# A long convolution rebuilt as a pipeline over 5 channel blocks, with taps as diagonal matmuls and a router that stays on the chip

## The chip, the cores and the metric

The kernel runs on one core of one Trainium2 chip. The engines of a core work side by side, each in its own program order: TensorE (PE, matmuls into PSUM), VectorE (DVE), ScalarE (ACT), GpSimd (POOL) and SyncE (SP, which here only issues DMAs). They wait for one another by semaphores. The metric is the device time of one execution in microseconds (us); the kernel before took 339.98 us, the median of 3 runs (338.54 to 340.74).

## The reference, cut to what matters

There are 2048 tokens of 640 channels, bf16. Part A is a gated long convolution between two modulated layer norms, part B a small expert that is applied to the 8 tokens with the highest router score.

```python
mod = (_silu(c) @ w_mod)                    # six vectors: sa, ca, ga, sb, cb, gb
h = _layernorm(x) * (1 + ca) + sa           # x = A_q
# part A
for t in range(4):                          # 4 shift taps along the tokens
    k_shift += k_pad[:, t:t + S, :] * shift_k[:, 3 - t]
kv = k_shift * v
y  = irfft(rfft(pad(kv)) * rfft(pad(ssm_k)))[:S] + kv * ssm_D   # length 4096, per channel
x = x + ga * (h * y)
h = _layernorm(x) * (1 + cb) + sb
# part B
r = h @ w_r;  idx = the 8 largest r
y = (silu(h[idx] @ w_gate) * (h[idx] @ w_up)) @ w_down * sigmoid(r[idx])
x = x + gb * (h + scatter_add(y, idx))
```

## The kernel before

Tokens lie 16 to a partition (`(p m) d`), so a full array is `[128, 16, 640]` bf16, 20 KB a partition. All big arrays share one pool of 7 such slots (tag `b20`). A scheduler orders each engine's instructions by their dependences and the slots; DMAs go out from SP's queue, the expert's weights and the last scatter from POOL's.

The Fourier transform of length 4096 is done in two steps of matmuls with a transposition through DRAM between them, for two halves of 320 channels. The sine tables `Cf`, `Sf` are made on the chip (L116 to L149) and transposed on PE (L156). `modv`, the six modulation vectors on all partitions, comes from 40 matmuls (L214). `ssm_k` is turned around through DRAM (`Gd`, `gL`, L282 to L286).

`kv` is made on DVE alone (L357 to L367): for each of 16 token groups four products with a tap, three sums and the product with `v`. `F1` (L288) is the first transform step: 64 matmuls a source, evicted by ACT with a rearrangement into `gZS` or `ZS`. `T1` (L298) stores that to `Zd` in DRAM and loads it back with a DMA transpose. `F3` (L306) is the second step, evicted by ACT and DVE. The spectra X and H are multiplied on DVE, 24 operations a half (L436 to L441). `I1` and `I2` (L324, L340) are the inverse steps. The first layer norm makes `h` on DVE (L393 to L415) beside the second half of the transforms; `h` goes to DRAM (`h_scr`) and comes back.

Then the tail: x1 = x + h*y (L461, L462), `layernorm` (L229) with sums on ACT and the rest on DVE and ACT, the router scores on DVE (L472), written to DRAM and read back as one row of 2048 on one partition, `max` and `max_index` there (L486, L488), the one-hot selection by matmuls (L514), the two projections (L529), the down projection (L550), the output on DVE (L561, L562), two stores, and an indirect DMA that adds the 8 rows to the stored output.

Of the kernel before, what the change touches and what calls it, by code (L numbers as in the profile page):

```python
# [19 lines left out]
M2 = 16  # L20
FF = 1728
NSEL = 8
NFFT = 4096
EPS = 1e-5
HB = 40
HC = 320


def _kernel_body(ctx, tc, A_q, A_k, A_v, A_shift_k, A_ssm_k, A_ssm_D,
                 B_w_r, B_w_gate, B_w_up, B_w_down, c, w_mod, out, dbg=None):  # L30
    nc = tc.nc
    dbg = dbg or {}

    def dump(name, ap):
        if name in dbg:
            nc.sync.dma_start(out=dbg[name], in_=ap)

    const = ctx.enter_context(tc.tile_pool(name="const", bufs=1))
    small = ctx.enter_context(tc.tile_pool(name="small", bufs=2))
    one = ctx.enter_context(tc.tile_pool(name="one", bufs=1))  # L40
    big = ctx.enter_context(tc.tile_pool(name="big", bufs=7))
    psum = ctx.enter_context(tc.tile_pool(name="psum", bufs=4, space=bass.MemoryType.PSUM))
    psum2 = ctx.enter_context(tc.tile_pool(name="psum2", bufs=2, space=bass.MemoryType.PSUM))
    dram = ctx.enter_context(tc.tile_pool(name="dram", bufs=1, space=bass.MemoryType.DRAM))

    def B20(name, shape, dtype=BF):
        n = 1
        for s_ in shape[1:]:
            n *= s_
        assert n * mybir.dt.size(dtype) <= 20480, (name, shape)  # L50
        return big.tile(list(shape), dtype, name=name, tag="b20")

    xq_d = A_q.flatten_outer_dims().rearrange("(p m) d -> p m d", p=P)
    k_d = A_k.flatten_outer_dims()
    k_d3 = k_d.rearrange("(p m) d -> p m d", p=P)
    v_d = A_v.flatten_outer_dims().rearrange("(p m) d -> p m d", p=P)
    out_d = out.flatten_outer_dims().rearrange("(p m) d -> p m d", p=P)

    cT = const.tile([P, 5], F32, name="cT")
    cT_bf = one.tile([P, 5], BF, name="cT_bf")  # L60
    D5 = one.tile([P, 5], BF, name="D5")
    with nc.allow_non_contiguous_dma(reason="tiny transposed loads"):
        nc.sync.dma_start(out=cT_bf[:], in_=c.rearrange("o (t p) -> p (o t)", p=P))
        nc.sync.dma_start(out=D5[:], in_=A_ssm_D.rearrange("(q r) -> q r", r=5))
    shk_bc = one.tile([P, 4, D], BF, name="shk_bc")
    kh = one.tile([P, 3, D], BF, name="kh")
    wr_bc = const.tile([P, D], BF, name="wr_bc")
    nc.sync.dma_start(out=wr_bc[:], in_=B_w_r.partition_broadcast(P))
    nc.vector.tensor_copy(out=cT[:], in_=cT_bf[:])

    trig_slot = B20("trig_slot", [P, 10240])
    trig_t = trig_slot[:, 0:5120].bitcast(F32).rearrange("p (a b) -> p a b", a=5)
# [563 lines left out]
```

## Time and profile before

| | |
|---|---|
| median of 3 runs | 339.98 us (338.54 to 340.74) |
| profiled execution, from its first to its last instruction | 336.5 us |
| mean granted clock of TensorE | 0.744 |
| DMA packets | 59888, 60.23 MB, mean 179 GB/s |

The slices of the page cut the span into 40 pieces; here are the other engines, the granted clock and the DMA share in tenths.

```profile
PE   0004900005776688929407795077500000002962
ACT  3111678004998598715403495024899677000000
POOL 5110000000000000000000000021000000000001
PEclk9999965555999569976957998559965555555859
DMA  6999382759167999999109703479910000000330
```

Four stretches can be read from them. Up to about 57 us, tables, loads and modulation; from there to 157 us the taps and the forward transforms; to 237 us products and inverse transforms; from then on the tail, in which PE and the DMA engines are nearly idle until 308 us.

### The profile page before, as it was taken

What the parts mean: (1) busy time and instruction counts of PE and PEld (TensorE: products, weight loads), DVE (VectorE), ACT (ScalarE), POOL (GpSimd) and SP (SyncE); (2) the same over time, 40 slices, a digit from 0 to 9 for tenths busy, and PEclk for the clock granted to TensorE, in tenths of its full rate; (3) what the DMA queues carried; (4) which work ended last, traced back from release to release, by engine and by line L of the source; (5) the groups of instructions that cost most, each with busy time, mean ns of one, the idle gap of its engine ahead of it and who ended that gap; (6) DMA issues with size and microseconds to landing.
All of it is one profiled execution on the core that took longest, in us unless ns stands there. A gap on an engine that the chain in (4) does not pass through costs nothing.

```text
span 336.5 us, 2691 instructions
## 1 busy us (share of the span) xinstructions
PE 137.7 (41%) x811; PEld 75.4 (22%) x811; DVE 248.5 (74%) x582; ACT 157.0 (47%) x275; POOL 11.7 (3%) x24
## 2 busy tenths in 40 slices
PE   0004900005776688929407795077500000002962
PEld 0002400002332234403106652056300000001631
DVE  5999880999999504897994429955860499999832
ACT  3111678004998598715403495024899677000000
POOL 5110000000000000000000000021000000000001
PEclk9999965555999569976957998559965555555859
DMA  6999382759167999999109703479910000000330
GB/s 219 431 405 428 152 297 93 263 118 204 80 253 307 240 289 258 345 257 392 78 0 161 152 1 111 202 263 406 381 51 0 0 0 1 0 1 3 156 158 1
DMA packets 59888, 60.23 MB, mean 179 GB/s; under 512 B 52906, under 2 KB 55090, under 8 KB 57698
## 3 DMA queue, kind: packets, MB, share of 16 engines
q1 hardware_dynamic: 58706, 53.42, 49.7%
q0 software_dynamic: 1168, 6.65, 5.1%
q8 instruction: 6, 0.10, 0.1%
q14 instruction: 8, 0.07, 0.1%
HBM read 28.59 MB, written 18.36 MB: 140 GB/s over the span
## 4 chain that ended last, share of the span: by engine, by line
DVE 54%; PE 16%; ACT 10%; DMA 9%; issue 6%; another core or an unknown queue 3%; SPq 1%; POOLq 1%; DVEq 0%
DVE ks_acc L366 6%; DVE ks_prod L365 6%; DVE acc_junk L472 4%; ACT ln_junk L235 3%; DMA xq<-in_A_q_dram 3%; PE ps_i L331 2%; PE ps_i L330 2%; DMA gZT<-Zd 2%; DMA ZT<-Zd 2%; PE pxs L514 2%; DVE ks_acc L362 2%; DVE ln_t L271 2%; DVE h L272 2%; DVE kv L367 2%
## 5 line engine op out<-in xcount | busy, mean ns | idle before, releaser
L330 PE MATMUL ps_i<-RA,Y 128*128 128x256 bf16 x80 | 21.6, 308 | 27.0 <-DVE Y L438 24.0
L336 ACT CAST UT<-ps_i 128x512 bf16<-128x512 f32 x20 | 11.7, 586 | 43.7 <-PE ps_i L331 27.8
L493 PE MATMUL pbc<-mif,ones 1*128 1x8 f32 x2 | 0.6, 351 | 67.3 <-DVE mif L490 67.3
L292 PE MATMUL ps_f<-gL,Cf 128*128 128x320 bf16 x32 | 10.8, 338 | 41.3 <-DMA gL<-Gd 36.6
L296 ACT CAST gZS<-ps_f 128x640 bf16<-128x640 f32 x32 | 19.8, 693 | 14.4 <-PE ps_f L293 14.4
L338 DVE CAST UT<-ps_i 128x512 bf16<-128x512 f32 x20 | 13.8, 692 | 14.9 <-ACT UT L336 14.9
L331 PE MATMUL ps_i<-RB,Y 128*128 128x256 bf16 x80 | 21.5, 308 | 3.6 <-DVE Y L441 3.6
L366 DVE TENSOR_TENSOR ks_acc<-ks_acc,ks_prod 128x640 bf16<-128x640 bf16 x48 | 22.9, 481 | 0.0
L296 ACT CAST ZS<-ps_f 128x640 bf16<-128x640 f32 x32 | 20.2, 693 | 5.2 <-PE ps_f L293 5.2
L365 DVE TENSOR_TENSOR ks_prod<-kt,shk_bc 128x640 bf16<-128x640 bf16 x45 | 20.4, 481 | 0.0
L320 DVE CAST H<-ps_f3i 128x480 bf16<-128x480 f32 (+1 forms) x12 | 7.5, 625 | 17.0 <-PE ps_f3i L318 17.0
L293 PEld LDWEIGHTS <-Sf 128*128 128x128 bf16 x64 | 6.5, 101 | 59.4 <-issue 59.2
L315 ACT CAST X<-ps_f3r 128x480 bf16<-128x480 f32 (+1 forms) x22 | 12.2, 554 | 11.7 <-PE ps_f3r L314 10.7
L330 PEld LDWEIGHTS <-Y 128*128 128x128 bf16 x80 | 11.7, 148 | 25.4 <-DVE Y L438 24.7
L493 PEld LDWEIGHTS pbc<-mif,ones 1*128 1x128 f32 x2 | 0.5, 304 | 67.6 <-issue 67.6
L269 ACT ACTIVATE ln_t<-ln_t,ln_rs 128x640 bf16<-128x640 bf16 x16 | 13.1, 827 | 5.2 <-DVE ln_t L266 3.7
L292 PE MATMUL ps_f<-kv,Cf 128*128 128x320 bf16 x32 | 11.6, 361 | 8.1 <-DVE kv L367 4.3
L320 DVE CAST X<-ps_f3i 128x480 bf16<-128x480 f32 (+1 forms) x12 | 7.5, 624 | 9.7 <-PE ps_f3i L318 9.7
L331 PEld LDWEIGHTS <-Y 128*128 128x128 bf16 x80 | 11.8, 148 | 9.9 <-issue 4.7
L315 ACT CAST H<-ps_f3r 128x480 bf16<-128x480 f32 (+1 forms) x22 | 12.2, 558 | 3.7 <-issue 2.0
L156 PE MATMUL pt_trig<-ident,Cf 128*128 128x128 bf16 x16 | 2.2, 286 | 27.4 <-ACT Cf L130 27.4
L348 ACT ACTIVATE ys<-ps_i 128x640 bf16<-128x640 f32 x16 | 10.4, 701 | 3.9 <-PE ps_i L346 3.9
(188 smaller groups left out, 479.0 us busy)
## 6 DMA issues: line engine op xcount, KB each, us to landing
xq<-in_A_q_dram SPq DMA_DIRECT2D x2, 2560.0 KB, 10.1
Zd<-gZS SPq DMA_DIRECT2D x4, 1280.0 KB, 4.8
Zd<-ZS SPq DMA_DIRECT2D x4, 1280.0 KB, 5.8
g_sb<-in_A_ssm_k_dram SPq DMA_DIRECT2D x1, 2560.0 KB, 16.1
kt<-in_A_k_dram SPq DMA_DIRECT2D x1, 2560.0 KB, 33.0
vt<-in_A_v_dram SPq DMA_DIRECT2D x1, 2560.0 KB
Gd<-g SPq DMA_DIRECT2D x1, 2560.0 KB, 14.3
h_scr<-h SPq DMA_DIRECT2D x1, 2560.0 KB, 7.5
```

The source lines that it names most:

```text
L269: nc.scalar.activation(out=t4[:], in_=t1[:], func=ACT.Copy, scale=rs[:, m:m + 1])
L292: nc.tensor.matmul(ps[:, 0, 0:HC], lhsT=Cf[:, m2, :], rhs=src[:, m2, col0:col0 + HC], start=True, stop=True)
L296: nc.scalar.copy(out=o_ap, in_=i_ap)
L315: nc.scalar.copy(out=dst[:, 0, k0:k0 + nk, :].rearrange("p a b -> p (a b)"), in_=psr[:, 0:ncol])
L320: nc.vector.tensor_copy(out=dst[:, 1, k0:k0 + nk, :].rearrange("p a b -> p (a b)"), in_=psi[:, 0:ncol])
L330: nc.tensor.matmul(o, lhsT=Yt[:, 0, :, blk], rhs=RA[:].rearrange("p a b -> p (a b)"), start=True, stop=False)
L331: nc.tensor.matmul(o, lhsT=Yt[:, 1, :, blk], rhs=RB[:].rearrange("p a b -> p (a b)"), start=False, stop=True)
L336: nc.scalar.copy(out=o_ap, in_=i_ap)
L338: nc.vector.tensor_copy(out=o_ap, in_=i_ap)
L365: nc.vector.tensor_tensor(out=prod[:], in0=src, in1=shk_bc[:, j, :], op=ALU.mult)
L366: nc.vector.tensor_tensor(out=acc[:], in0=acc[:], in1=prod[:], op=ALU.add)
L472: nc.vector.scalar_tensor_tensor(out=junk[:], in0=h2[:, m, :], scalar=1.0, in1=wr_bc[:], op0=ALU.mult, op1=ALU.mult, accum_out=r32[:, m:m ...
```

## The change

The program is written anew. Channels go in 5 blocks of 128 (`NB`), tokens along the free dimension for the taps (`kT`, `vT`, loaded by DMA transpose, two for each block) and 128 tokens to a partition group for the norms (`(m p) d`). SP's and POOL's instructions keep the order in which they are written; the scheduler still orders PE, DVE and ACT.

For a block `b`, `conv(b)` makes the taps as 16 matmuls of 512 columns with diagonal matrices that hold a tap, and DVE multiplies the PSUM result by `vT`. The block goes to DRAM and comes back in another order (`kvd`, `xA`). `stage_A` and `stage_B` are the two transform steps, for two sources at a time that share one pair of buffers `A` and `HX`: g0 with g1, g2 with kv0, g3 with kv1, g4 with kv2, kv3 with kv4. `product` multiplies two spectra in place with 12 DVE operations. `stage_BT` and `stage_AT` are the inverse steps, with a trip through DRAM (`Ud`, `uA`) between them. `stage_AT` adds h*y to x, and takes the statistics and the router score of the block at once, the score by transposing x on PE and multiplying it by two columns of weights. Norm and score are finished when all blocks are in. `Balance` gives a set share of the PSUM evictions to DVE and the rest to ACT. PSUM is one pool of four buffers of two banks. `HX` has three buffers, which in turn hold the angles for the tables, the spectra and a part of `w_mod`; another part of `w_mod` lies where x is loaded later.

The top 8 are found for 16 groups of 128 tokens on 16 partitions, and the 128 candidates are ranked by comparisons; nothing of it goes through DRAM. The output is summed on PE by three matmuls with the identity and evicted by ACT.

```diff
-        nc.vector.tensor_tensor(out=kv[:, m, :], in0=acc[:], in1=vt[:, m, :], op=ALU.mult)
+    ctx.enter_context(tc.manual_schedule(engines={mybir.EngineType.SP, mybir.EngineType.Pool}))
+    psum = ctx.enter_context(tc.tile_pool(name="psum", bufs=4, space=bass.MemoryType.PSUM))
...
+    def conv(b):
+        for i2 in range(2):
+            ps = ps_tile([P, 2, 512])
+            for i in range(2):
+                n0 = 16 + 512 * (2 * i2 + i)
+                for j in range(4):
+                    nc.tensor.matmul(ps[:, i, :], lhsT=diag_b(b)[:, j, :], rhs=kT[:, n0 - j:n0 - j + 512],
+                                     start=(j == 0), stop=(j == 3))
+            V.tensor_tensor(out=kvT[:, 1024 * i2:1024 * i2 + 1024], in0=ps[:].rearrange("p a b -> p (a b)"),
+                            in1=vT[:, 1024 * i2:1024 * i2 + 1024], op=ALU.mult)
+        nc.gpsimd.dma_start(out=kvd[:], in_=kvT[:])
...
+    def stage_A(src, A, u):
+        for g4 in range(4):
+            ps = ps_tile([P, 2, 32, 16])
+            for bb in range(4):
+                nc.tensor.matmul(ps[:, bb // 2, :, (bb % 2) * 8:(bb % 2) * 8 + 8], lhsT=src[:, 4 * g4 + bb, :],
+                                 rhs=RA[:].rearrange("p k c e -> p (k c) e"), start=True, stop=True)
+            bal.copy(o, ps[:])
+    def stage_B(A, HX):
+        for kk in range(8):
...
+                nc.tensor.matmul(ps[:, i, :], lhsT=FT[:, 0, k2, :], rhs=f(A[:, 2 * k2:2 * k2 + 2]),
+                                 start=True, stop=False)
...
+            bal.copy(HX[:, 2 * kk:2 * kk + 2].rearrange("p k c u d -> p (k c u d)"),
+                     ps[:].rearrange("p a b -> p (a b)"))
+    def product(xt, ux, ht, uh):
+        for hk in range(2):
...
+            V.tensor_tensor(out=t0, in0=Xr, in1=Hr, op=ALU.mult)
+            V.tensor_tensor(out=t1, in0=Xi, in1=Hi, op=ALU.mult)
+            V.tensor_tensor(out=t2, in0=Xr, in1=Hi, op=ALU.mult)
+            V.tensor_tensor(out=Xi, in0=Xi, in1=Hr, op=ALU.mult)
+            V.tensor_tensor(out=Xr, in0=t0, in1=t1, op=ALU.subtract)
+            V.tensor_tensor(out=Xi, in0=Xi, in1=t2, op=ALU.add)
...
+    def stage_AT(b):
+        for hb in range(2):
...
+            V.tensor_tensor(out=t[:].rearrange("p m (g j) -> p m g j", g=2), in0=ps[:].rearrange("p g m j -> p m g j"),
+                            in1=h[:, :, cc].rearrange("p m (g j) -> p m g j", g=2), op=ALU.mult)
+            V.tensor_tensor(out=xq[:, :, cc], in0=xq[:, :, cc], in1=t[:], op=ALU.add)
+        for m in range(M):
+            V.bn_stats(out=st2[:, m, b, :], in_=xq[:, m, c0:c0 + P])
...
+        for m in range(M):
+            nc.tensor.matmul(pr[:, m, :], lhsT=xT[:, m, :], rhs=wcol[:, b, :], start=True, stop=True)
...
+    product(X1, 1, X0, 0)
+    stage_B(A2, X2)
+    stage_BT(X1, 1, 0)
...
+    product(X2, 1, X0, 1)
+    stage_B(A3, X3)
+    stage_BT(X2, 1, 1)
+    load_uA(1)
+    stage_AT(0)
+    A4, X4 = As(), HXs()
+    stage_A(kvAs[3], A4, 0)
+    stage_A(kvAs[4], A4, 1)
+    product(X3, 1, X1, 0)
+    stage_B(A4, X4)
...
+            for hf in range(2):
+                cc = slice(hf * 320, hf * 320 + 320)
+                nc.tensor.matmul(po[:, hf, 0:320], lhsT=ident[:], rhs=gbs[:, cc], start=True, stop=False)
+                nc.tensor.matmul(po[:, hf, 0:320], lhsT=ident[:], rhs=xq[:, m, cc], start=False, stop=False)
+                nc.tensor.matmul(po[:, hf, 0:320], lhsT=ident[:], rhs=tm[:, i, cc], start=False, stop=True)
+            nc.scalar.copy(out=xq[:, m, :].rearrange("p (h d) -> p h d", h=2), in_=po[:, :, 0:320])
```

Two places of the new order matter for what follows. The first is DVE's order where spectra are multiplied. Before, in the first half of the channels (T and Y are the products' buffers, X and H the spectra), the products stand by themselves:

```order
L437 TENSOR_TENSOR T_1208<-X_1118,H_786 128x1280
L439 TENSOR_TENSOR T_1208<-X_1118,H_786 128x1280
L440 TENSOR_TENSOR T_1208<-X_1118,H_786 128x1280
L438 TENSOR_TENSOR Y_1207<-T_1208 128x1280
L441 TENSOR_TENSOR Y_1207<-T_1208 128x1280
```

Now, in the product of spectra 2 and 0 (`HX_622` and `HX_170`; `Ta` and `Tb` are its buffers, `rs1` and `nm1` the norm's scale and shift, `n1a` and `n1i` steps of the scale):

```order
L265 TENSOR_TENSOR HX_622<-HX_622,Tb_760 128x8x128
L476 SCALAR_TENSOR_TENSOR nm1_954<-mv1_889,rs1_938 128x16
L260 TENSOR_TENSOR Ta_759<-HX_622,HX_170 128x1024
L479 TENSOR_SCALAR h_956<-xq_164,rs1_938,nm1_954 128x640 x16
L483 TENSOR_TENSOR h_956<-h_956,modv_163 128x2560 x2
L484 TENSOR_TENSOR h_956<-h_956,modv_163 128x2560 x2
```

All of h (16 operations, and 8 large ones, of which the last four follow below these rows) has moved between the first operation of the product's second half and its other five.

The second place is SP's queue at the loads. Before, all inputs but three go out one behind the other:

```order
L77 DMA xq_88<-in_A_q_dram 128x10240
L79 DMA g_sb_90<-in_A_ssm_k_dram 128x10240
L85 DMA wmodA_92<-in_w_mod_dram 128x5x1920
L86 DMA wmodB_93<-in_w_mod_dram 128x5x1920
L89 DMA kt_96<-in_A_k_dram 128x10240
```

Now (`wmx` and `early` are the other homes of `w_mod`, `kvd1` and `kvd2` blocks of kv in DRAM):

```order
L320 DMA xA_347<-kvd1_274 128x16x128
L338 DMA early_74<-in_w_mod_dram 128x5x640 x2
L338 DMA wmx_427<-in_w_mod_dram 128x5x640 x2
L338 DMA xq_164<-in_w_mod_dram 128x5x640 x2
L95 DMA gA_434<-in_A_ssm_k_dram 128x16x128
L83 DMA_TRANSPOSE kT_436<-in_A_k_dram 128x2048
L84 DMA_TRANSPOSE vT_437<-in_A_v_dram 128x2048
L320 DMA xA_441<-kvd2_425 128x16x128
L413 DMA xq_164<-in_A_q_dram 128x4x640 x4
```

The loads of x, once among the first, have moved behind `w_mod`, whose last two parts occupy their buffer, and behind a kv block that comes back from DRAM.

1024 lines of the change are left out of this document (530 added, 494 removed).

## The prediction

> **What bounds the kernel now.** I read the page's busy shares, the slices, the chain, then the chain in order of time and groups by form, and last the windows of the two stages that the change rebuilds.
>
> ```profile
> span 336.5 us, 2691 instructions
> PE 137.7 (41%) x811; PEld 75.4 (22%) x811; DVE 248.5 (74%) x582; ACT 157.0 (47%) x275; POOL 11.7 (3%) x24
> DVE  5999880999999504897994429955860499999832
> DVE 54%; PE 16%; ACT 10%; DMA 9%; issue 6%; another core or an unknown queue 3%; SPq 1%; POOLq 1%; DVEq 0%
> 57.00:66.00 9.00, 0.00 (x0) 0.00 (x0) 7.38 (x20) 1.09 (x2) 0.00 (x0) 0.50 0.83 299
> 75.00:84.00 9.00, 4.66 (x16) 1.98 (x16) 9.00 (x23) 3.99 (x7) 0.00 (x0) 0.50 1.01 214
> 127.00:135.00 8.00, 6.19 (x32) 3.04 (x31) 4.13 (x8) 5.93 (x13) 0.00 (x0) 1.00 1.21 262
> ```
>
> The reader is to see that VectorE (DVE) is the bound: 248.5 us busy of 336.5, 54% of the chain. The window rows give busy time of PE, weight loads, DVE, ACT, POOL, then the granted clock, the DMA share and GB/s.
>
> The change is judged by pricing its rows from these durations (start, length, what; then groups, with mean ns):
>
> ```profile
> 58.80 0.80 DVE ks_prod L365 x2
> 162.56 0.57 DVE X L320
> 165.73 0.73 DVE T L436
> 122.78 1.29 ACT ZS L296 x2
> L401 DVE BATCH_NORM_STATS2 ln_stats<-xq 128x6 f32<-128x320 bf16 x16 | 7.7, 478 | 0.0
> L402 DVE BATCH_NORM_AGGREGATE ln_mv<-ln_stats 128x2 f32<-128x12 f32 x16 | 3.1, 197 | 0.0
> 137.20 0.44 DVE L411 TENSOR_SCALAR ln_tn<-xq,ln_rstd,ln_nmr 128x640 bf16<-128x640 bf16 x1
> 137.55 0.48 DVE L415 TENSOR_TENSOR h<-ln_t,sg 128x640 bf16<-128x640 bf16 x1
> L280 DVE COPY g<-g_sb 128x2048 bf16<-128x2048 bf16 x2 | 3.9, 1995 | 0.0
> 266.64 0.17 DVE L255 TENSOR_TENSOR ln_q<-ln_t,ln_r 128x16 f32<-128x16 f32 x1
> 266.85 0.17 DVE L257 TENSOR_TENSOR ln_s<-ln_q,ln_s 128x16 f32<-128x16 f32 x1
> 184.02 0.27 PE L330 MATMUL ps_i<-RA,Y 128*128 128x256 bf16 x1
> 184.13 0.27 PE L331 MATMUL ps_i<-RB,Y 128*128 128x256 bf16 x1
> 179.64 0.42 PE L330 MATMUL ps_i<-RA,Y 128*128 128x256 bf16 x1
> 179.85 0.42 PE L331 MATMUL ps_i<-RB,Y 128*128 128x256 bf16 x1
> 317.54 2.02 PE L529 MATMUL pp_gT<-x_selT,w_gate_sb 128*128 128x8 bf16 x70 [0.27 <-DVE x_selT L521]
> ```
>
> Prices as start-to-start times. A two-operand DVE row on 640 bf16 costs 0.40 us (two in 0.80), on 1280 0.73, so 0.60 on 1024 and 1.40 on 2560. A DVE read of PSUM: 0.57 for 480, so 1.14 for 1024. ACT from PSUM: 0.645 for 640, so 0.97 for 1024, an estimate by the same slope. Statistics of 320: 0.39 after the overlap of 0.08 seen on the other rows; of 128: 0.19 by the same slope. Aggregate 0.13, two-scalar row on 640 0.35 (137.20 to 137.55), a small row that hangs on the one before 0.21. A 256-column matmul: 0.11 at clock 1, 0.21 at 0.5; 16 of them 1.75. A matmul of 8 columns: 2.02/70 = 0.029.
>
> **The change part by part.**
>
> *Removed.* The shift taps on DVE: 64 products with taps, 48 sums and 16 products with v, 128 rows at 0.40, 51 us. They become 80 matmuls of 512 columns (80 x 0.215 = 17 us of PE) and ten DVE products from PSUM (11.4 us). The second normalisation's 16 ACT pairs and its three DVE passes, and the accumulating router rows, go too:
>
> ```profile
> L235 ACT ACTIVATE ln_junk<-xq 128x640 bf16<-128x640 bf16 x16 | 11.6, 723 | 0.0
> L472 DVE SCALAR_TENSOR_TENSOR acc_junk<-h,wr_bc 128x640 bf16<-128x640 bf16 x16 | 12.1, 816 | 0.0
> L486 DVE MAX8 m<-rrow_t 1x8 f32<-1x2048 f32 x1 | 2.3, 2274 | 0.0
> ```
>
> In their place stand per block 16 statistics rows, 16 transposes and 16 two-column matmuls, and top 8 on 16 partitions x 128 instead of 1 x 2048.
>
> *All DVE rows of the new program*, priced so, come to 181 us against 248.5: evictions 26, products 60 x 0.60 = 36, first normalisation 14.6 + 17.0, five output blocks 34, the taps 11.4, tables, router and rest 42. ACT: about 79 evictions x 0.97 + 38 = 115 us. PE: 302,000 columns at 0.11/256 us = 130 us at clock 1. So DVE stays the longest engine, but no engine fills the span; the sum goes along the path.
>
> *A, start to the modulations, 60 us.* First table and first tap data at 10 (DVE's first 26 rows 6-7 us behind a first landing like the 2.7 to 3.5 us below). Then PE in its order, each step the slower of its matmuls and the evictions: four short transforms 4 x 2.9 (three ACT evictions each), four convolutions 4 x 3.5, three sine rows of ACT in the way 3, two long transforms 2 x 6.8, modulation 60 x 0.135 = 8.1: 50. DMA beside it: eight transposes, three 0.5 MB loads of g, the first kv trips, w_mod:
>
> ```profile
> 3.51 1.40 DVE L69 CAST cT<-cT_bf 128x5 f32<-128x5 bf16 x1 [3.51 <-DMA cT_bf<-in_c_dram]
> 71.01 9.94 SPq L285 DMA_TRANSPOSE gL<-Gd  x2
> wmodA<-in_w_mod_dram SPq DMA_DIRECT2D x1, 2400.0 KB, 21.6
> xq<-in_A_q_dram SPq DMA_DIRECT2D x2, 2560.0 KB, 10.1
> h_scr<-h SPq DMA_DIRECT2D x1, 2560.0 KB, 7.5
> h_re<-h_scr SPq DMA_DIRECT2D x1, 2560.0 KB, 10.5
> ```
>
> A 2560 KB transpose pair kept the SP queue 9.94 us, so 512 KB 2 us and eight 16; w_mod 21.6 as long as one half landed; the rest 5.2 MB at 10 us per 2.5 MB, 21: 59 us if nothing overlaps, 40 if they do. It is hidden by PE's 60, barely; what is late next is the modulation. Ends 46 and 72; I take 60.
> The weight on DMA has a rule against it: the Trainium skill, DMA: Bandwidth & Descriptors, section Specifications, wants at least 512 bytes in a transfer for line rate, and the loads of g and kv go in runs of 256. The trace moved its transposes, also in small packets, at 214 GB/s with the engines full, against 299 for large ones, so I keep the measured price. The rule names no rate below its bound; were it half of 214, the six such loads (3 MB, 14 us at 214) would add 14 us, an estimate, and the sum would be 272 at most.
>
> *B, the block inputs, 4 us.* x is loaded into the buffer that held w_mod, so its four loads stand on SP behind the modulation's matmuls; a quarter of 10.1 plus latency: 4.
>
> *C, DVE from the first statistics row to the last output block, 139 us.* In DVE's order the rows sum to 118.8: statistics 32 x 0.39 + 16 x 0.13 = 14.6; products 36; h 16 x 0.36 + 8 x 1.40 = 17; evictions 11.6 with the tables' and x's transposes; two tap products 2.3; five blocks each 2 x 1.14 + 2 x 0.60 + 16 x 0.19 + 0.3 = 6.8, 34; small rows 3.3. Waits on top, 20: taps of block 4 are behind the modulation on PE (4). The spectrum of block 3 takes the buffer of spectrum 0, freed only by the last product with it, and DVE has put all of h in the middle of that product; ACT's eight evictions (7.8) start then, and DVE needs the first four: 5. The block after waits for transposes, two short transforms and four evictions behind the first output block on in-order PE: 8. The last uA round trip (1 MB out, 1 MB in: 3 + 4 from the rows above) lies under two output blocks, 13.6 us: 3. Below nothing for the waits is excluded by the order; above, each could double: 0 to 40.
> *D, the tail, 52 us.* Aggregates 2, 16 small rows 3.4, 11 rows of xn 4, router 9 (fourteen small rows, four 0.73 rows that the scheduler put between them, three trips to PE), select 80 x 0.029 = 2.4 and 0.8, two projections 4.1 and 0.6, down projection 28 x 0.135 to 0.27, 5, then 96 matmuls of 320 for the output, 96 x 0.135 = 13, last ACT 0.7, last store 4, indirect add 4.2 (332.30 to the end of the span):
>
> ```profile
> 192.67 0.30 PE L345 MATMUL ps_i<-UT,Cb 128*128 128x320 bf16 x1
> 192.80 0.30 PE L346 MATMUL ps_i<-UT,Sb 128*128 128x320 bf16 x1
> 324.63 5.90 PE L550 MATMUL py<-w_down_sb,hT 128*8 128x320 bf16 x28 [3.00 <-DVE hT L544]
> 320.35 5.31 DMA out_dram<-ob
> 332.30 1.47 POOL L567 DMA_INDIRECT out_dram<-delta,idx  x1 [96.10 <-DVE delta L557]
> ```
>
> The new order puts the output matmuls behind the down projection, and the indirect add behind all four stores: 17.7 us that before lay beside the router. Ends: 44 with the output at ACT's pace alone, 65 with PE at half clock there.
>
> Sum: 60 + 4 + 139 + 52 = 255 us of span. Profiled execution 336.5, median 339.98: 3.5 around it, which stay: **258 us**.
>
> **Clock.** PE was granted 0.50 where it waited for data (57 to 84) and 1.00 where matmuls were dense (127 to 135); 256 columns took 0.21 and 0.11. I take 1 except in the tail's down projection.
> The Trainium skill, TensorE: Matmul & The Clock Gate, Part 1, says that an idle window of about 3.4 us halves the clock and a busy one restores it. The rows agree in kind; by it PE, which here waits for DVE in stages C and D, would be cold for most of them, and that is the second rival.
>
> **The rivals.**
> 1. *The waits of C are hidden and A is shorter.* For it: PE and ACT both have slack in C. Against: DVE's order. 258 - 20 - 5 = about 233.
> 2. *Half clock makes PE the bound.* PE's 39 units of 16 x 256 columns after the modulation cost 68 us at 0.11 and 134 at 0.21; half of the difference on the path, 33 us: 291. For it: 0.50 in three stretches above. Against: 1.00 wherever matmuls were denser than now.
> 3. *DVE rows on strided blocks lose the fast rate.* L280, with a step between elements, took 1995 ns for 2048, twice the time per element of ks_prod. If products, output blocks and h went so: 60 x 0.53 + 8 x 1.33 + 10 x 0.53 = 48, so 306. Against: the runs inside a row are 64 or more elements without a step.
> 4. *The round trips through DRAM are exposed: slower.* Ten trips (five of kv, five of U) hang on one in-order SP queue, behind transposes that wait for PE. With the 7.5 + 10.5 of h_scr and h_re for each, a trip is 18; if 10.5 of it showed each time, 258 + 105 - 13 of waits counted already = 350. It decides from 82/9 = some 9 us a trip. Against: each trip here is 0.5 or 1 MB, and its reader comes a block later.
> 5. *The pipeline doesn't overlap, so DVE's saving is all there is:* 340 - 67 = 273; with PE's added columns (302,000 against 227,000 by the kernel before, 75,000 at 0.11/256 us) serial on top, 305. For it: only four PSUM buffers, shared by all stages. Against: PE, DVE and ACT work on different blocks in the order that is written.
>
> **How the numbers follow.** Forecast (243 to 275) 0.55, rival 1 0.14, rival 2 0.14, rival 3 0.06, rival 4 0.05, rival 5 0.06. The time is the likeliest case's, 258. The range 236 to 298 takes in the forecast, rival 2 and most of rival 1; a third of rival 1, half of 5, and 3 and 4 lie outside, 0.19. Within 1% (337 to 343) is no change that can be told: 0.02, from the far end of 5 and the near one of 4; slower 0.05, rival 4; faster 0.93.
>
> **What would show it.** Step A: the first x load issues near 60 us. B and C: DVE at 90% or more from 64 to about 200 with two gaps of 4 to 10 us at the products with spectra 3 and 4 (ACT named). Product rows 0.60 apart. D: the output matmuls start only after the down projection, 18 us before the end. Wrong would be: gaps on DVE that name a DMA of xA or uA (rival 4), product rows above 0.9 us (rival 3), PEclk 5 through C with PE full (rival 2).

## The result, and the profile after

The new kernel takes 273.27 us, the median of 4 runs (272.77 to 273.75), beside 340.10 us for the kernel before on the same chip: a ratio of 0.806, 95% interval 0.802 to 0.809. The profiled execution has a span of 271.1 us and a time of 272.9. In all that follows, ratios leave out the slow executions of a kernel (over 1.5% above its fastest) while medians in us do not, and the profiled executions of e3 and e4 are slow ones.

The first fence is the page of the new kernel: engines, three rows of slices, the chain's shares.

```profile
span 271.1 us, 3680 instructions
PE 164.4 (61%) x1428; PEld 116.6 (43%) x1428; DVE 182.0 (67%) x443; ACT 114.3 (42%) x124; POOL 15.5 (6%) x40
DVE  5159965762477999999969219977867899502300
PEclk9999997999999965786588699959955755558995
DMA  8960999999999210500004400534889770000450
PE 38%; DVE 34%; DMA 10%; issue 10%; ACT 3%; POOL 1%; POOLq 1%; SPq 0%; DVEq 0%; ACTq 0%
```

DVE is still the longest engine, but no longer the chain's main part: 34% instead of 54. The slices show where the span isn't DVE's: the first quarter, in which the DMA engines are full, the dent after 150 us, the last fifth.

The windows of the four stages follow (start:end, length, busy time of PE, weight loads, DVE, ACT, POOL, granted clock, DMA share, GB/s): the start, the rest of stage A with B, stage C, stage D. The DMA share adds up the times of single packets, so it can come out above 1.

```profile
0.00:16.35 16.35, 0.00 (x0) 0.00 (x0) 4.84 (x22) 1.79 (x3) 3.98 (x17) 1.00 1.11 180
16.35:76.25 59.90, 53.89 (x331) 33.92 (x332) 40.05 (x71) 35.40 (x39) 2.75 (x7) 0.97 0.92 238
76.25:218.00 141.75, 83.58 (x741) 63.53 (x740) 116.43 (x271) 61.37 (x59) 7.37 (x15) 0.78 0.43 137
218.00:271.10 53.10, 26.98 (x364) 19.16 (x361) 20.66 (x81) 15.70 (x23) 1.44 (x1) 0.66 0.22 75
```

A and B together took 76.25 us where 64 were forecast, C 141.7 against 139 (116.4 of DVE rows and 25.3 of waits, against 118.8 and 20), D 53.1 against 52. DVE's sum, 182.0, met the 181 forecast.

Stage A in order of time (start, length, what; in brackets the idle time before it and what ended it):

```profile
4.71 4.45 ACTq L132 DMA_DIRECT2D cT_bf<-in_c_dram  x1
15.81 0.21 ACT L342 ACTIVATE silu_c<-cT_bf 128x5 bf16<-128x5 bf16 x1 [3.56 <-DMA cT_bf<-in_c_dram]
18.12 3.49 PE L229 MATMUL ps<-RA,gA 128*128 128x256 bf16 x16 [18.12 <-DVE gA L324]
40.95 0.23 DVE L324 TENSOR_TENSOR gA<-gA,Dt 128x16 bf16<-128x16 bf16 x1 [2.32 <-DMA gA<-in_A_ssm_k_dram]
55.93 10.73 SPq L83 DMA_TRANSPOSE kT<-in_A_k_dram  x1
60.54 2.88 PE L349 MATMUL ps<-early 128*128 128x320 bf16 x20
69.64 3.08 SPq L413 DMA_DIRECT2D xq<-in_A_q_dram  x4
76.25 0.89 DVE L471 BATCH_NORM_STATS2 st<-xq 128x6 f32<-128x320 bf16 x2 [3.35 <-DMA xq<-in_A_q_dram]
```

ACT issued two loads of g, and the issue of the small load of c behind them held the engine for 4.45 us; it landed at 15.8, and the scheduler had put the silu that needs it ahead of the first sine, from which the short table of PE's first matmul is made. So PE began at 18.1, not at 10. From there to the modulation it took 42.4 us; the forecast's steps sum to 42.2, but 3.0 of the 42.4 are a wait of PE for block 2 of g (the DVE row at 40.95), which the forecast didn't have. Then x: its loads were issued at 69.64, one us after the modulation's end and behind a transpose that had held SP's queue for 10.7 us, and their first row came 6.6 us later.

DVE's largest waits in C, the start of the next product row, and the start of stage D:

```profile
139.07 0.69 DVE L260 TENSOR_TENSOR Ta<-HX 128x1024 bf16<-128x1024 bf16 x1 [2.13 <-ACT HX L46]
155.66 1.23 DVE L44 CAST A<-ps 128x1024 bf16<-128x1024 f32 x1 [4.85 <-PE ps L229]
162.91 0.69 DVE L260 TENSOR_TENSOR Ta<-HX 128x1024 bf16<-128x1024 bf16 x1 [6.03 <-ACT HX L46]
163.52 0.68 DVE L261 TENSOR_TENSOR Ta<-HX 128x1024 bf16<-128x1024 bf16 x1
217.89 0.57 DVE L570 BATCH_NORM_AGGREGATE mv<-st 128x2 f32<-128x30 f32 x3
```

The waits stand where the forecast put them, and product rows start 0.61 us apart. The 4.85 and the 6.03 are one chain, which PE's rows of the same time show:

```profile
146.83 1.16 PE L401 MATMUL ps<-ident,xq 128*128 128x128 bf16 x16 [3.56 <-DVE xq L396]
149.99 0.59 PE L406 MATMUL ps<-wcol,xT 128*128 128x2 bf16 x16 [2.00 <-ACT xT L46]
150.44 5.62 PE L229 MATMUL ps<-RA,xA 128*128 128x256 bf16 x32
158.05 0.38 PE L240 MATMUL ps<-A,FT 128*128 128x512 bf16 x1 [2.00 <-ACT A L46]
```

PE waits for the first output block's sum (3.56), transposes it, waits for ACT's copy (2.00), computes the score, and only then starts the short transforms of kv3 and kv4 and, at 158, the long one.

### The profile page after: what moved, and what is told of

It reads as the page before. It is cut to its first block, busy times and chain, and to the rows that moved or that the text cites. A ratio compares the mean times of both kernels' runs of the same rounds, so it can differ in the third digit from the quotient of the medians.

```text
span 271.1 us, 3680 instructions
## 1 busy us (share of the span) xinstructions
PE 164.4 (61%) x1428; PEld 116.6 (43%) x1428; DVE 182.0 (67%) x443; ACT 114.3 (42%) x124; POOL 15.5 (6%) x40
## 4 chain that ended last, share of the span: by engine, by line
PE 38%; DVE 34%; DMA 10%; issue 10%; ACT 3%; POOL 1%; POOLq 1%; SPq 0%; DVEq 0%; ACTq 0%
PE ps L389 4%; DVE st L471 4%; PE ps L240 4%; PE ps L229 4%; DMA kvd<-kvT 4%; DMA gA<-in_A_ssm_k_dram 3%; DVE t L394 3%; PE ps L349 3%; PE ps L307 3%; DMA xq<-in_A_q_dram 2%; PE ps L277 2%; PE ps L677 2%; PE ps L279 2%; DVE xq L396 2%; DVE h L479 2%
## 5 line engine op out<-in xcount | busy, mean ns | idle before, releaser
L240 PE MATMUL ps<-A,FT 128*128 128x512 bf16 x80 | 33.1, 414 | 18.8 <-ACT HX L46 12.7
L46 ACT CAST HX<-ps 128x1024 bf16<-128x1024 f32 x31 | 29.9, 1023 | 32.2 <-DVE HX L263 16.9
L46 ACT CAST A<-ps 128x1024 bf16<-128x1024 f32 x30 | 28.3, 1028 | 17.9 <-PE ps L229 17.9
L229 PE MATMUL ps<-RA,gA 128*128 128x256 bf16 x80 | 14.1, 349 | 21.4 <-DVE gA L324 21.1
L242 PE MATMUL ps<-A,FT 128*128 128x256 bf16 x80 | 23.4, 293 | 0.0
L244 PE MATMUL ps<-A,FT 128*128 128x256 bf16 x80 | 23.4, 293 | 0.0
L277 PE MATMUL ps<-IT,HX 128*128 128x256 bf16 x80 | 19.8, 289 | 2.5 <-DVE HX L264 2.3
L46 ACT CAST U<-ps 128x1024 bf16<-128x1024 f32 x18 | 17.4, 1020 | 8.6 <-PE ps L279 8.0
L279 PE MATMUL ps<-IT,HX 128*128 128x256 bf16 x80 | 19.4, 289 | 0.5 <-DVE HX L265 0.5
L44 DVE CAST A<-ps 128x1024 bf16<-128x1024 f32 x10 | 12.1, 1222 | 10.9 <-PE ps L229 10.9
L307 PE MATMUL ps<-kT,early 128*128 128x512 bf16 x80 | 18.1, 379 | 0.4 <-ACT A L46 0.4
L242 PEld LDWEIGHTS <-FT 128*128 128x128 bf16 x80 | 8.4, 105 | 20.1 <-issue 18.4
L398 DVE BATCH_NORM_STATS2 st<-xq 128x6 f32<-128x128 bf16 x80 | 16.0, 280 | 0.1
L244 PEld LDWEIGHTS <-FT 128*128 128x128 bf16 x80 | 8.4, 105 | 11.2 <-issue 3.0
```

Source lines behind the costliest of these rows:

```text
L46: self.nc.scalar.copy(out=out, in_=in_)
L229: nc.tensor.matmul(ps[:, bb // 2, :, (bb % 2) * 8:(bb % 2) * 8 + 8], lhsT=src[:, 4 * g4 + bb, :], rhs=RA[:].rearrange("p k c e -> p (k c) ...
L240: nc.tensor.matmul(ps[:, i, :], lhsT=FT[:, 0, k2, :], rhs=f(A[:, 2 * k2:2 * k2 + 2]), start=True, stop=False)
L242: nc.tensor.matmul(ps[:, i, 0:256], lhsT=FT[:, 1, k2, :], rhs=f(A[:, 2 * k2 + 1:2 * k2 + 2]), start=False, stop=False)
L244: nc.tensor.matmul(ps[:, i, 256:512], lhsT=FT[:, 2, k2, :], rhs=f(A[:, 2 * k2:2 * k2 + 1]), start=False, stop=True)
L277: nc.tensor.matmul(ps[:, i, :], lhsT=xt[:, k2, 0, ux, :], rhs=IT[:, k2, 1:3, :].rearrange("p a b -> p (a b)"), start=True, stop=False)
```

## The experiments

Each kernel ran beside the kernel before, on several chips, on which that took 339.8 to 341.6 us; so ratios are compared. "Against new" is the difference of the ratios times 340 us. The three columns of stages are from the profiled executions.

| run | us, median | ratio (95%) | against new | first matmul | first statistics row | span |
|---|---|---|---|---|---|---|
| new kernel | 273.27 | 0.806 (0.802-0.809) | | 18.12 | 76.25 | 271.1 |
| e1_start | 274.92 | 0.808 (0.803-0.813) | +0.6 | 16.61 | 76.35 | 272.0 |
| e2_x_early | 281.06 | 0.823 (0.816-0.830) | +6 | 17.85 | 77.93 | 278.9 |
| e3_a4_first | 272.75 | 0.798 (0.791-0.804) | -2.8 | 18.28 | 77.82 | 273.3 |
| e4_out_spread | 266.55 | 0.777 (0.771-0.783) | -10 | 18.06 | 79.33 | 267.5 |
| e5_share0 | 270.88 | 0.795 (0.790-0.800) | -3.6 | 18.19 | 78.20 | 269.5 |
| e6_taps_dve | 290.98 | 0.852 (0.844-0.860) | +16 | 18.26 | 89.64 | 288.3 |
| e7_loads_early | 275.90 | 0.813 (0.808-0.818) | +2.4 | 15.28 | 73.49 | 272.6 |
| e8_score_later | 257.03 | 0.756 (0.752-0.759) | -17 | 18.33 | 77.21 | 254.8 |
| e9_long_runs | 271.43 | 0.796 (0.789-0.803) | -3.3 | 15.96 | 75.60 | 270.9 |
| e10_later_spread | 249.27 | 0.730 (0.724-0.736) | -26 | 18.22 | 78.89 | 247.1 |
| e11_later_spread_share0 | 248.11 | 0.729 (0.724-0.734) | -26 | 18.07 | 76.79 | 243.9 |
| e12_all | 246.17 | 0.727 (0.723-0.732) | -27 | 15.12 | 72.52 | 242.4 |

In seven of these kernels stage A is the same program (new, e3, e4, e5, e8, e10, e11), and the first statistics row lies between 76.25 and 79.33 (78.89 without e3 and e4): from one kernel's profile to the next, stage A alone scatters by some 3 us.

### Stage A: the start, x, and the loads

```diff
-        load_g(0, nc.scalar)
+        nc.scalar.dma_start(out=cT_bf[:], in_=c.rearrange("o (t p) -> p (o t)", p=P))
+        nc.scalar.dma_start(out=wr_c[:], in_=B_w_r.rearrange("(t p) -> p t", p=P))
...
         nc.scalar.dma_start(out=Dt_rows, in_=D_rows)
+        load_g(0, nc.scalar)
         load_g(1, nc.scalar)
...
```

> Edit: on ScalarE's DMA queue the small loads of c, w_r and D are issued ahead of the two loads of g. In the new kernel the load of c was issued at 4.71 us behind the two loads of g, its issue held ScalarE for 4.45 us, the table load of ScalarE came at 10.97, the silu of c at 15.81 after the 11.1 us landing, and the first short sine and the first matmul (18.12) stood behind it. Theory (the start is 8 us late because ScalarE's queue was held and c landed late, and TensorE's path from there to the modulations passes it on): first matmul at about 12, when the first block of g has landed (3.5 + 8.3), the first statistics row about 6 earlier, 273.3 - 6 = 267. Rival (stage A is bound by its loads, DMA share 0.92 from 16 to 76 us, and the two last parts of w_mod landed at about 65, just before they were read): first matmul at 12 all the same, but the modulations come only 0 to 2 us earlier, 271 to 273, and TensorE waits for w_mod or the second block of g instead.

The silu came at 12.0 instead of 15.8, but the first matmul only 1.5 us earlier: the scheduler, which orders ACT's DMA issues too, had left the load of D behind g, and now its issue was held for 4.74 us. By block 2 of g, which had landed at 40.7 as before, the gain was gone. That is the rival's outcome.

```diff
-        for a, wm in enumerate(homes):
+        for a in (4, 5, 0, 1, 2, 3):
...
-        nc.sync.dma_start(out=xq[:, 4 * q:4 * q + 4, :], ...)
+        nc.gpsimd.dma_start(out=xq[:, 4 * q:4 * q + 4, :], ...)
```

> Edit: the two parts of w_mod that lie in x's buffer are loaded and multiplied first, and the four loads of x are issued on POOL's queue instead of SP's, where they stood behind kT4, whose issue held the queue from 55.9 to 66.7. x can then be loaded after 20 of the modulation's 60 matmuls, about 63.5 instead of 69.6. Theory (VectorE bounds the stage from the first statistics row on, so that what lets it begin brings the end forward): first statistics row at about 70.5, 5 us earlier, and 268. Rival (the pace there is TensorE's and ScalarE's, whose work starts after the modulation as before): the first row is at 70.5, but VectorE waits as much more for the taps of block 4 and the products' spectra, and the time stays within 1 us of 273.

Both were wrong, and the run doesn't tell them apart. The second short table is computed in a scratch that lies in the home of the first part of w_mod, and that part was now loaded third instead of first. DVE's and PE's rows in e2:

```profile
56.00 0.48 DVE L178 TENSOR_SCALAR early<-arow,mc 128x128 f32<-128x128 f32 x2 [5.71 <-DMA early<-in_w_mod_dram]
58.00 0.59 PE L240 MATMUL ps<-A,FT 128*128 128x512 bf16 x1 [4.63 <-DVE HX L44]
77.93 1.28 DVE L472 BATCH_NORM_STATS2 st<-xq 128x6 f32<-128x320 bf16 x3 [9.82 <-DMA xq<-in_A_q_dram]
```

A small DVE row waited 5.7 us for a load, the evictions stood behind it, and PE behind those; x was issued at 69.0 all the same, and its first row came 8.9 us later.

The row points at more than a wait. In the new kernel it runs here:

```profile
51.47 0.47 DVE L178 TENSOR_SCALAR early<-arow,mc 128x128 f32<-128x128 f32 x2
```

The two parts of w_mod that lie in `early` were issued from 43.07 on and landed 7.5 us after their issue, and PE reads them from 60.54. The first lies in `early[:, 2560:5760]`, the table's scratch in `early[:, 2560:5120]`. So the table writes over weights that are still to be read, and a part of `sa` comes out of them. That is a mistake in the order in which the new kernel is written; only e12, which computes the table ahead of the loads, is free of it.

The next run moves loads into the gap that SP's queue had from 15 to 25 us:

```diff
-        nc.scalar.dma_start(out=Dt_rows, in_=D_rows)
+        nc.gpsimd.dma_start(out=Dt_rows, in_=D_rows)
...
     load_kv(1)
+    load_g(2)
+    load_wm(4, xf[:, 0:3200])
+    load_wm(5, xf[:, 3200:6400])
```

> Edit: at the start c and w_r are loaded ahead of g on ScalarE's queue, D on POOL's; block 2 of g and the two parts of w_mod that lie in x's buffer are issued on SP behind the first two blocks of k and v, at about 15 us, where SP's queue stands still until 25.7 and the DMA engines until 27. The kernel with only the small loads moved won 1.5 us at the first matmul (D's load had stayed behind g) and nothing at the end. Theory (the order of the queues, not bandwidth, holds stage A): first matmul at 12.5 instead of 18.1, no wait for block 2 of g (3.0), the modulations 5 to 9 us earlier, 264 to 268. Rival (DMA bandwidth holds it: share 1.11 to 16 us, 0.92 to 76): the transposes land later by what was put in front of them, and the time stays within 2 us of 273.

DVE's and PE's rows on the way to the modulation, in e7:

```profile
18.78 0.23 DVE L335 TENSOR_TENSOR gA<-gA,Dt 128x16 bf16<-128x16 bf16 x1 [3.55 <-DMA gA<-in_A_ssm_k_dram]
51.07 0.48 DVE L189 TENSOR_SCALAR early<-arow,mc 128x128 f32<-128x128 f32 x2 [3.95 <-DMA early<-in_w_mod_dram]
60.95 0.23 DVE L335 TENSOR_TENSOR gA<-gA,Dt 128x16 bf16<-128x16 bf16 x1 [2.18 <-DMA gA<-in_A_ssm_k_dram]
62.55 2.88 PE L355 MATMUL ps<-early 128*128 128x320 bf16 x20
```

PE began 2.8 us earlier and reached the modulation 2 us later: three landings took it back, one of them (3.95) again at the table's row in the home of w_mod, which comes from the order of writing (e12 does without it). x was issued at 69.40, about as before, but its first row came after 4.1 us instead of 6.6, so the first statistics row was 2.8 us earlier. Nothing of that reached the end: from there to the start of D the kernel took 144.9 us instead of 141.6. The time is near the rival's; what in stage C takes back an earlier x was not tested, but the modulation, and with it PE's steps behind it, came 2 us later.

Is it the short runs of 256 bytes? The next run reads g and kv with one run of 4096 bytes for each partition:

```diff
-        (eng or nc.sync).dma_start(out=gA[:], in_=rows_ap(A_ssm_k, b, S_TOK, P))
+        (eng or nc.sync).dma_start(out=gA[:].rearrange("p m q -> p (m q)"),
+                                   in_=A_ssm_k.flatten_outer_dims()[b * P:(b + 1) * P, :])
...
-        nc.sync.dma_start(out=xA[:], in_=rows_ap(kvd[:], 0, S_TOK, P))
+        nc.sync.dma_start(out=xA[:].rearrange("p m q -> p (m q)"), in_=kvd[:])
```

> Edit on the new kernel: the five loads of g and the five of the kv blocks read each partition's 4096 bytes in one run instead of 16 runs of 256 bytes; the order of the tokens inside a block, and with it the convolution's result, is left out. In the new kernel such a load of g landed after 8.3 us (0.5 MB) and seven of the ten lie ahead of the first statistics row, with the DMA engines at a share of 1.11 and 0.92. Theory (short runs cost the DMA engines about twice their time, and the loads hold stage A): seven times 1.4 us of 16 engines, half of 0.5 MB at 180 GB/s, less, the load of c is no longer held up, the first matmul at 11 to 13 instead of 18.1, no wait for block 2 of g, the first statistics row 7 to 10 us earlier: 263 to 267. Rival (transposes and TensorE's 42 us of steps hold it): the first matmul is earlier, but the waits move to the transposes, 270 to 273.

The loads of g on SP's and ACT's queue (number, KB, us to landing), in the new kernel:

```profile
gA<-in_A_ssm_k_dram SPq DMA_DIRECT2D x3, 512.0 KB, 8.4
gA<-in_A_ssm_k_dram ACTq DMA_DIRECT2D x2, 512.0 KB, 8.3
```

In e9:

```profile
gA<-in_A_ssm_k_dram SPq DMA_DIRECT2D x3, 512.0 KB, 7.2
gA<-in_A_ssm_k_dram ACTq DMA_DIRECT2D x2, 512.0 KB, 5.7
```

The windows of the start and the rest of stage A in e9:

```profile
0.00:16.35 16.35, 0.39 (x2) 0.28 (x3) 6.46 (x29) 2.40 (x4) 3.91 (x17) 1.00 0.98 193
16.35:76.25 59.90, 51.80 (x308) 31.98 (x310) 37.31 (x65) 31.63 (x36) 2.75 (x7) 0.94 0.90 230
```

The load of c was no longer held (its issue took 0.55 us), but the DMA share fell only from 1.11 to 0.98 and from 0.92 to 0.90, that is 0.13 x 16.35 + 0.02 x 59.9 = 3.3 us of the DMA engines' time, not 10. The time, 271.4, is the rival's, but the waits did not go to the transposes: DVE waited 4.07 us for block 2 of g, and then once more at the table's row, with PE behind it:

```profile
50.08 0.48 DVE L179 TENSOR_SCALAR early<-arow,mc 128x128 f32<-128x128 f32 x2 [5.85 <-DMA early<-in_w_mod_dram]
52.87 0.59 PE L241 MATMUL ps<-A,FT 128*128 128x512 bf16 x1 [4.10 <-DVE kvT L310]
```

The modulation began at 64.64 instead of 60.54, although the first matmul came 2.2 us earlier. So long runs were worth some 3 us here, and what they would bring without that wait is open. The run also prices the rule which the prediction weighed (the Trainium skill, DMA: Bandwidth & Descriptors, Specifications, at least 512 bytes for line rate): the trace agrees that shorter runs cost something, and the 14 us that a halved rate would have meant are not there.

### Stage C: what ends DVE's waits

```diff
-    stage_AT(0)
     A4, X4 = As(), HXs()
     stage_A(kvAs[3], A4, 0)
     stage_A(kvAs[4], A4, 1)
+    stage_AT(0)
```

> Edit: the short transforms of kv3 and kv4 are written ahead of the first output block instead of behind it. In the new kernel VectorE waited 4.85 + 6.03 = 10.9 us there (151 to 163 us) for TensorE, which had 16 transposes, 16 two-column matmuls and the short transforms to do in order behind the output block. Theory: with the order exchanged the wait is covered by the output block's VectorE rows (6.9 us), and 5 to 9 us go: 264 to 268. Rival (the spectra of block 4 are late because of ScalarE's 8 evictions and the third spectrum buffer, not because of TensorE's order): the wait comes back at the product with spectrum 3 and the time stays within 2 us of 273.

The wait of 4.85 became 2.46, the 2.13 became 0.58, but the one at the product with the last spectrum was 6.64 instead of 6.03: its long transform still stood on PE behind the score of the first output block. The time fell by 2.8 us, with intervals that overlap, and not by 5 to 9; it is near the rival's, and the edit leaves open which of the two causes holds. The score was then taken out of the block and written later:

```diff
+    def score(b):
+        c0 = b * P
         pt = ps_tile([P, M, P], BF)
...
     stage_B(A4, X4)
+    score(0)
...
     stage_AT(3)
+    score(2)
     stage_AT(4)
+    score(3)
+    score(4)
```

> Edit: the short transforms of kv3 and kv4 are written ahead of the first output block, and the score of an output block (16 transposes, a copy by ScalarE, 16 two-column matmuls, VectorE's sum) behind the next large step of TensorE instead of inside the block. With the short transforms alone moved, the wait of 10.9 us became 2.5 + 6.6, since the long transform of kv3 and kv4 still stood on TensorE behind the score, which waits for VectorE's sums and ScalarE's copy (155.97). Theory (TensorE's order makes that wait): the 6.6 and the waits of 1.5 and 1.6 ahead of the last two output blocks go, 8 to 10 us, 263 to 265. Rival (ScalarE's evictions into the freed spectrum buffer make it): the product with spectrum 4 still waits 5 us or more, 269 to 272.

DVE's two largest waits in e8 from 110 us to the end of the stage:

```profile
147.09 1.22 DVE L44 CAST A<-ps 128x1024 bf16<-128x1024 f32 x1 [2.51 <-PE ps L229]
181.23 2.36 DVE L394 TENSOR_TENSOR t<-ps,h 128x1024 bf16<-128x1024 f32 x2 [2.48 <-PE ps L389]
```

The start of the long transform of kv3 and kv4 on PE:

```profile
149.20 0.38 PE L240 MATMUL ps<-A,FT 128*128 128x512 bf16 x1
```

The window of stage C:

```profile
77.21:202.49 125.28, 77.72 (x732) 60.22 (x733) 115.45 (x271) 60.15 (x59) 7.36 (x15) 0.82 0.46 149
```

The long transform starts at 149.2 instead of 158.05, the product with its spectrum no longer waits, and the stage takes 125.3 us instead of 141.7 with the same DVE rows: 9.8 of waits instead of 25.3. The gain is 17, twice what was expected, since most of the waits at the later blocks went too (9.4 us in all from 178 us on in the new kernel, 2.5 in e8). The theory holds: ACT makes the same evictions as before (60.2 us busy in the stage instead of 61.4), and the wait at the product is gone. Since e3 alone won 2.8 us, about 14 come from the scores. The Trainium skill says in TensorE: Matmul & The Clock Gate, Part 3, The mechanism, that matmuls start and end strictly in program order; the trace agrees: 16 transposes of 1.16 us in all, with what they wait for, held a transform up that doesn't need them.

```diff
-    bal.share = 0.125
+    bal.share = 0.0
```

> Edit: from the products on, the eviction share of VectorE is 0 instead of 0.125, so some eight PSUM evictions (1.14 us apart, 9 us) go from VectorE to ScalarE (0.94 apart), which is busy 61.4 us of the 141.8 from the first statistics row to the last output block. Theory (VectorE bounds that stage, 116.4 us busy of 141.8): 5 to 9 us go, 264 to 268. Rival (the stage is set by the waits, and each of them ends with a ScalarE eviction: 2.13, 6.03, 2.41): the waits grow by what VectorE no longer does, 272 to 275.

DVE's busy time in C fell by 7.7 us (116.4 to 108.7 in the same window), the time by some 3.6: half of what DVE was given was taken back by waits, the largest 13.02 at the product with the last spectrum, where the 4.85 and the 6.03 of the new kernel have run together. The time lies between the two expectations, as it would if DVE's rows counted in part of the stage and PE's order in the rest.

### The taps themselves

```diff
+        tk = ring.tile([P, 2, 1024], BF, name="tk", tag="V", bufs=2)
...
+            V.tensor_scalar(out=o, in0=kT[:, n0:n0 + 1024], scalar1=shk_f[:, b, 0:1], scalar2=None, op0=ALU.mult)
+            for j in range(1, 4):
+                V.tensor_scalar(out=tk[:, j % 2], in0=kT[:, n0 - j:n0 - j + 1024], scalar1=shk_f[:, b, j:j + 1], scalar2=None,
+                                op0=ALU.mult)
+                V.tensor_tensor(out=o, in0=o, in1=tk[:, j % 2], op=ALU.add)
+            V.tensor_tensor(out=o, in0=o, in1=vT[:, 1024 * i2:1024 * i2 + 1024], op=ALU.mult)
```

> Edit: the shift taps are put back on VectorE, for each half of a block four products with a tap, three sums and the product with v on 1024 bf16 instead of 8 matmuls of 512 columns and one product from PSUM; the diagonal matrices are not built. VectorE has per block 8 x 0.5 + 8 x 0.60 = 8.8 us instead of 2.4 and 1 for the diagonals, TensorE 16 x 0.215 = 3.4 less. Theory (in stage A TensorE sets the pace, busy 54 of 60 us, VectorE 40): four blocks add 4 x 5.4 = 22 to VectorE's 40 and take 14 from TensorE's 54, so VectorE takes over with 62 and A is 2 to 8 us longer, the fifth block adds 5 to 6 behind it: 280 to 287. Rival (stage A is bound by its loads and queue, so the taps' place is free there): only the fifth block shows, 273 to 279. Second rival (TensorE's release is worth more than VectorE's load): below 270.

The engines' busy times on the page of e6:

```profile
PE 153.2 (53%) x1343; PEld 112.0 (39%) x1348; DVE 207.4 (72%) x493; ACT 114.0 (40%) x124; POOL 15.7 (5%) x40
```

Its sums and tap products (busy, mean ns; idle time before them):

```profile
L307 DVE TENSOR_TENSOR kvT<-kvT,tk 128x1024 bf16<-128x1024 bf16 x30 | 20.6, 686 | 0.3
L305 DVE TENSOR_SCALAR tk<-kT,shk_f 128x1024 bf16<-128x1024 bf16 x30 | 13.8, 482 | 7.8 <-DMA kvd<-kvT 7.7
```

DVE has 25.4 us more, PE 11.2 less, stage A ends 13 us later, and the time is 16 us longer: the theory's direction, beyond its range. Of the 16 us, up to 7.7 are waits that the edit made itself, since its temporary takes one of the two buffers of kv. So the matmuls are worth 8 to 16 us here, less than the 25 that they take off DVE.

### Stage D, and the sum of what helped

```diff
+    def out_pair(m2):
+        tm = ring.tile([P, 2, D], BF, name="tm", tag="K")
...
+    out_pair(0)
+    out_pair(1)
     pc_ = ps_tile([P, 2, P])
...
     pg = proj(wg)
...
+    out_pair(6)
+    out_pair(7)
     pu = proj(wu)
```

> Edit: the output's eight pieces (each 12 matmuls of 320 columns, one VectorE row of 0.73 to 0.80, two ScalarE evictions of 0.69) are written into the gaps of the router and of the expert instead of behind the down projection: two before the candidates' broadcast, one each before the one-hot and the selection, two before the gate projection, two before the up projection. In the new kernel TensorE does next to nothing from 218 to 234, and 22.9 us follow the down projection: 13 of output matmuls, the last eviction, a store and the indirect add. Theory: 13 us behind the down projection go, the pieces that don't fit a gap cost 5 before it and the four VectorE rows that come earlier up to 3, and the down projection runs at a higher granted clock (6.2 us for 28 matmuls at 0.50, 3.8 at 1): 10 less, 263. Rival (the router is bound by VectorE and TensorE's order delays it by what is taken off the end): the down projection ends 10 to 13 us later than 248.2 and the time stays within 2 us of 273.

The down projection and the indirect add in the new kernel:

```profile
242.01 6.22 PE L677 MATMUL ps<-wd,hT 128*8 128x320 bf16 x28 [0.43 <-DVE hT L666]
...
266.39 1.44 POOL L701 DMA_INDIRECT out_dram<-delta,idx  x1 [52.11 <-issue]
```

The down projection and the add in e4:

```profile
257.63 3.97 PE L702 MATMUL ps<-wd,hT 128*8 128x320 bf16 x28 [0.43 <-DVE hT L691]
...
262.83 1.44 POOL L710 DMA_INDIRECT out_dram<-delta,idx  x1 [43.42 <-DVE delta L705]
```

In the new kernel the indirect add came 18 us behind the down projection, in e4 1.2 behind it. Counted from the start of stage D (217.89 and 223.01) the down projection began 10.5 us later, ran 2.25 faster, and the stage took 44.5 us instead of 53.2. The theory held, with its price: the down projection ended 8.2 us later, counted so, and the time fell by some 10 us all the same.

> Edit: the score of an output block and the short transforms of kv3 and kv4 in TensorE's other order (257.0 by itself), and the output's pieces spread over router and expert (7 to 10 us by itself). Theory (they lie in different stages and add): 247 to 250. Rival (the spread pieces meet the scores that were put off, both on TensorE and ScalarE behind the last output block): 251 to 255.

> Edit: as the run with the later scores and the spread output, and in addition no PSUM eviction on VectorE from the products on. By itself that won 3 us of the 9 that left VectorE, since waits on TensorE and ScalarE took the rest. Theory (with TensorE's order mended VectorE bounds the stage, 9.7 us of waits are left of 23): 5 to 8 us below the run without it. Rival (the remaining waits are ScalarE's evictions, which grow): within 2 us of it.

The two edits added up (249.3), as the theory of e10 has it. Taking the evictions from DVE as well changed the ratio by 0.001, far inside the intervals, which is the rival of e11: freeing DVE of rows alone wins nothing measurable there.

> Edit: the fastest version so far (248.1; scores later, output spread, no evictions on VectorE from the products on) with the loads issued early at the start, and the second short table computed ahead of the loads of w_mod. With the early loads alone the first matmul came 2.8 us earlier, but three waits took it back on the way to the modulation: 3.4 behind the landing of block 1 of g, 2.9 behind the second short table, whose scratch lies in the buffer of a part of w_mod so that VectorE waited 3.95 for that load, and 2.2 for block 3 of g. Theory (the waits of stage A are made by order): without the second of them the first statistics row comes at 70 to 72 instead of 76.8, and 242 to 245. Rival (the loads hold the stage, above all the transposes, for which SP's queue stood still 5 to 11 us each): the wait goes to the next load, first row at 73.5 or later, 246 to 249.

e12 adds to e11 the early loads of e7, and computes the second short table ahead of the loads of w_mod. DVE's wait for g in e12:

```profile
61.70 0.23 DVE L335 TENSOR_TENSOR gA<-gA,Dt 128x16 bf16<-128x16 bf16 x1 [7.38 <-DMA gA<-in_A_ssm_k_dram]
```

DVE now waited 7.4 us for block 3 of g. Even so the first statistics row came 4.3 us earlier than in e11, at 72.5, between what the theory and the rival put there; but from there to the start of D the kernel took 126.0 us instead of e11's 122.3, so the ratio is not to be told from e11's. As in e7, what the start of C won was lost inside C, by what was not tested. With 246 to 249 us, e10 to e12 are the fastest versions: 0.73 of the kernel before.

## Why the prediction was right, and where it was not

The forecast of 258 us missed 273.3 by 15, inside its range and its likeliest case. The sum of the span was 255 against 271.1, and the time around it 2 instead of 3.5. All four stages came out longer than forecast (by 8.6, 3.6, 2.7 and 1.1 us), so the time fell at the upper end of the likeliest case.

- **DVE's rows: right.** 181 forecast, 182.0 measured; product rows 0.61 apart against 0.60. Rival 3, slow strided rows, is out: the rows show it. (Its price was also read too high: 1995 ns for 2048 elements is 1.6 times, not twice, the time per element of 0.40 us for 640.) The 1.14 us for a PSUM read of 1024 was partly luck: 0.57 for 480 gives 1.22 in proportion, which is what one such row lasts, and 1.13 is what two start apart.
- **A, 60 us: the mis-sized term, by 8.** The forecast put the first matmul at 10 and 42 us of steps behind it; that took 42.4, but began at 18.1. The agreement of the 42 is partly luck: 3 us were forecast for sine rows in PE's way, and in the trace PE waited for none of them, but 3.0 for block 2 of g. The new kernel's order has the load of c behind g and the silu ahead of the sine, and the prediction did not use it; that an issue can hold ACT for 4.45 us, none of the rows it read had shown. The forecast also said that DMA, 40 to 59 us, is hidden "barely". e1, e7 and e12 show how barely: PE started 1.5 to 3.0 us earlier, and on the way to the modulation landings took back all of it in e1 and e7. In e7 and e12 the first statistics row still came earlier, by 2.8 and 4.3 us, and then stage C was longer. So the late start is where the 8 us lie in this trace; that removing it would bring 8 is not shown, and of what was tried at the start only e9 shortened the time, by some 3 us.
- **B, 4 us: 7.6.** x was issued a little behind the modulation's end as forecast; the first row came 6.6 us behind the issue instead of 4, beside a transpose, g and kv. e2 tried to bring it forward and failed for another reason. In e7 and e12 the first row was earlier and the time was not, so the prediction's addition of B to C is itself in doubt: C doesn't simply begin with x.
- **C, 20 us of waits: 25.3, with other sizes.** The block behind the first output block was forecast with 8 and waited 4.85 + 6.03 = 10.9, by the mechanism given (in-order PE), as e3 and e8 show together. The product with the third block's spectrum, forecast with 5, waited 2.8 (0.62 + 2.13); for the taps of block 4, 4 were forecast; their two rows waited for nothing, and the 1.7 close to them is the product's buffer `Tb`, which had to wait for the store of kv. The rows of the later blocks were forecast with 3 and had 9.4: there the prediction looked for a DMA trip, and what DVE waited for were again PE's steps behind the scores, as the 2.5 in e8 show. DVE was busy 116.4 of 141.7 us, 82%, and not the 90% or more that were named as a sign.
- **D, 52 us: 53.1**, with its cause. The terms written there add up to 53.2, so that the miss of 1 is one of adding. e4 took 9 to 10 of the 17.7 us that the prediction said had been moved behind the down projection.
- **The other rivals.** Half clock (rival 2): the granted clock was 0.97 in A and 0.78 in C, where PE was busy 83.6 of 141.7, so PE's work did not bound; the lower clock cost 2.25 us at the down projection (6.22 against 3.97), and what it cost at the steps of C that DVE waited for was not measured. Exposed round trips (rival 4): no wait of DVE or PE in C names uA or xA. No overlap (rival 5) gave 273 as a number, but not as a mechanism: PE's and DVE's busy times sum to more than the span. Waits hidden (rival 1): e10 to e12 reach 246 to 249 that way, and the forecast of 233 for it needed the shorter A too.

## What to carry to other kernels

On an engine that works in order, look for small instructions that wait for two other engines and have a large step behind them that doesn't need them: here the scores of the output blocks, 16 short transposes and their products each, cost about 14 us, and writing them later took nothing else away (stage D 52.3 us instead of 53.2). Idle time that a trace puts down to one engine (ACT's evictions) can belong to what stands ahead on a third; an edit of the order decides it. Before removing a late start, ask what was in the meantime being loaded: where the DMA share was 0.9 and more, time won at the head came back here as the next landing, at a row whose scratch lay in the home of a load (e2, e7, e9), or as waits in the stage behind. A wait like that of the table's row also deserves a look for its own sake: it showed here a buffer that is written while its contents are still needed.

## What the runs showed of the hardware

The issue of a small DMA can hold its engine for microseconds when large loads of short runs stand ahead in the same queue: 1.2 KB took 4.45 us to issue behind two loads of g in runs of 256 bytes, 0.55 us when g came in runs of 4096. The hold moves to whatever is issued next (4.74 us for D's load in e1). And the issue of a transpose held SP's queue for up to 10.7 us while the DMA engines were full.
